# Twenty-one short and fourteen long dummy matmuls in the fill of a fused attention and ReGLU kernel, in place of four and twelve

## Chip, cores, metric

One core of a Trainium2 chip. The metric is the device time of one execution in microseconds (us). The kernel before was run four times: 345.63, 346.99, 349.79 and 351.38 us, median 348.39 us. The profiled execution is the one of 345.63 us.

## What is computed

The reference runs attention on a batch of 8 with 8 heads, 576 positions and 64 features, and feeds the result to a ReGLU feed-forward layer. Attention is the sum of a pooled part (queries, keys and values averaged over groups of 4 positions, full softmax over 144 pooled positions, each result repeated 4 times) and a local part (softmax over the keys less than 4 positions away).

```python
out_up = np.repeat(sm_attn(q_d, k_d, v_d), 4, axis=2)          # q_d, k_d, v_d: means over 4 positions
mask = np.abs(pos[:, None] - pos[None, :]) < 4
out_local = softmax(where(mask, scale * q @ k.T, -1e9)) @ v
x = (out_up + out_local).transpose(0, 2, 1, 3).reshape(4608, 512)
out = (np.maximum(x @ w_gate, 0) * (x @ w_val)) @ w_out        # 512 -> 1536 -> 512
```

## The kernel before

The work is cut into 32 head pairs (two heads of 64 features side by side, 128 rows) for attention and nine chunks of 512 tokens for the feed-forward layer. Each engine runs its instructions strictly in the order in which they are written. That order is not computed at build time: it is a list of words by hand or by a planner, `FRONT` for the fill (the first pairs, until the feed-forward work of chunk 0 can keep TensorE busy), `ORDER` for the repeated middle, `TAIL` for the end. Each word emits one step, and a step's last number is mostly the PSUM bank that it uses (there are eight).

The steps of the fill that matter here, for head pair p:

- `loadq/p`, `loadk/p`, `loadv/p`: the loads, issued by GpSimd (POOL). The first q alone is loaded by SyncE (SP) and cast by ScalarE (ACT).
- `tr/p/i/bank` (L364): TensorE (PE) turns q and k by multiplying with an identity; `ev/p/..A` or `..V` (L378) copies the result out of PSUM on ACT or VectorE (DVE).
- `vd/p/6` (L408): PE pools the values into bank 6, columns 0 to 255; `vc/p/6` (L417): ACT copies them out.
- `s1/p/b` (L427 pooled, L438 local): PE makes the scores in banks b to b+3; `ed/p` (L462) and `ex/p/g` (L448): ACT takes their exponentials; `ma/p/g` (L454): DVE applies the band mask.
- `sd/p/6` (L475): PE makes the pooled attention in bank 6, columns 0 to 259; `rd` (L499) and `td` (L504): DVE divides it into `xo`.
- `su/p/4` (L487): PE makes the local attention in banks 4 and 5; `ru` (L512) and `tu/p/g` (L518): DVE divides it into `xo`.
- `xp/p/g` (L622, L624): PE adds both parts, turned back; `xe` (L634) copies them to `xT`, the input of the feed-forward layer.
- `hg`, `hv` (L639): the first feed-forward matmuls, 128x512 each.
- `warm/n` (L812): n dummy matmuls on zeros. The short ones have 248 columns and write bank 6, columns 264 to 511, which nothing reads. The long ones, emitted once ahead of the list, have 512 columns and write bank 7.

A dummy has no data to wait for, but it does wait for the engines that were still to read its bank: the profile shows the first of the two dummies behind `td/0/6` waiting for that step's DVE instruction, though the columns differ.

Before, there are twelve long dummies at the very beginning, two short ones ahead of `tr/1/0/7` and two short ones ahead of `vd/1/6`.

## Time and profile before

| | |
|---|---|
| median of 4 runs | 348.39 us |
| lowest, highest | 345.63, 351.38 us |
| profiled execution | 345.63 us, of it a span of 343.9 us from the first to the last instruction |
| PE busy | 334.5 us, 3210 matmuls |
| DVE, ACT, POOL busy | 295.9, 218.0, 183.4 us |
| all L812 matmuls | 12 of 512 columns, 4 of 248 |
| PE waits of 0.2 us and more, 0 to 24 us | 4.9 us in eight waits |
| PE waits of 0.2 us and more, 24 to 344 us | 0.9 us in three waits |

A timeline row gives the start, the length from the first start to the last end, engine, source line, operation, tiles, shape, and the number of instructions merged into the row; in brackets stands how long the engine had been idle and what ended that. Matmuls overlap, so the distance between starts, not the length of one, is what a matmul costs in a stream. The PEclk row of the page is the clock that a throttle granted. It stands at 9 in every slice.

### The profile page before, as it was taken

How to read it: one execution, taken by the hardware profiler on the slowest of the kernel's cores; microseconds unless marked ns; L12 is line 12 of the kernel's file. 1: busy time of each engine (PE TensorE's matmuls, PEld its weight loads, DVE VectorE, ACT ScalarE, POOL GpSimd, SP SyncE). 2: the span in 40 equal slices, each digit the busy share in tenths (PEclk: the TensorE clock that was granted, in tenths of full speed). 3: DMA queues.
4: the chain of work that ended last, by engine and by line, in shares of the span. 5: the costliest groups of instructions: out<-in, count | busy, mean ns of one | idle time of the engine just before them, and what ended most of it. 6: DMA issues, size and time to landing. Idle time of an engine off the chain costs nothing.

```text
span 343.9 us, 8224 instructions
## 1 busy us (share of the span) xinstructions
PE 334.5 (97%) x3210; PEld 214.4 (62%) x3210; DVE 295.9 (86%) x546; ACT 218.0 (63%) x423; POOL 183.4 (53%) x232
## 2 busy tenths in 40 slices
PE   7789999999999999999999999999999999999996
PEld 3665556666475756575666556665766557768685
DVE  6695679988999999999999999899999798786892
ACT  4878767767767776677667767776677633334222
POOL 8986547686999695989296877840300000000000
PEclk9999999999999999999999999999999999999999
DMA  9999999999999999999989995992100001001023
GB/s 148 165 171 186 186 192 161 141 172 153 215 147 172 124 170 120 134 158 178 84 105 137 180 128 75 128 170 53 43 20 33 31 2 46 32 31 59 30 66 109
DMA packets 167974, 40.02 MB, mean 116 GB/s; under 512 B 149856, under 2 KB 164864, under 8 KB 167936
## 3 DMA queue, kind: packets, MB, share of 16 engines
q0 software_dynamic: 132160, 22.63, 92.9%
q1 hardware_dynamic: 35632, 16.84, 26.4%
q8 instruction: 25, 0.41, 0.5%
q14 instruction: 13, 0.11, 0.1%
q10 hardware_dynamic: 144, 0.03, 0.1%
HBM read 45.86 MB, written 9.44 MB: 161 GB/s over the span
## 4 chain that ended last, share of the span: by engine, by line
PE 90%; DVE 4%; DMA 2%; ACT 2%; issue 1%; POOL 1%; DVEq 0%; ACTq 0%; POOLq 0%
PE ps L639 48%; PE ps L724 23%; PE ps L905 4%; PE ps L585 4%; PE ps L438 2%; PE ps L427 2%; PE ps L593 2%; PE ps L364 2%; DMA qk<-in_q_dram 2%; PE ps L408 1%; DVE ee L454 1%; DVE gT L651 1%; DVE xn L612 1%; DVE xo L718 0%; DMA out_dram<-y_sb 0%
## 5 line engine op out<-in xcount | busy, mean ns | idle before, releaser
L639 PE MATMUL ps<-xT,wv_sb 128*128 128x512 f16 x432 | 109.1, 379 | 0.0
L639 PE MATMUL ps<-xT,wg_sb 128*128 128x512 f16 x352 | 88.4, 380 | 0.0
L648 ACT ACTIVATE r<-ps 128x512 f16<-128x512 f32 x88 | 52.0, 596 | 31.7 <-PE ps L639 29.2
L651 DVE TENSOR_TENSOR gT<-r,ps 128x512 f16<-128x512 f16 x88 | 59.1, 681 | 7.5 <-PE ps L639 4.7
L639 PEld LDWEIGHTS <-wv_sb 128*128 128x128 f16 x432 | 40.4, 98 | 39.7
L639 PEld LDWEIGHTS <-wg_sb 128*128 128x128 f16 x352 | 32.6, 98 | 32.3 <-issue 0.2
L612 DVE TENSOR_TENSOR xn<-ps,rden 64x720 f16<-64x720 f32 x48 | 43.4, 905 | 5.4 <-ACT rden L608 4.2
L603 ACT ACTIVATE rden<-ps 64x720 f32<-64x720 f32 x48 | 36.7, 764 | 14.4 <-PE ps L593 13.4
L448 ACT ACTIVATE ee<-ps 112x576 f16<-112x576 f32 x64 | 38.7, 647 | 6.0 <-PE ps L438 4.9
L309 POOL DMA_DIRECT2D qk<-in_k_dram x46 | 33.7, 738 | 10.3 <-DMA v<-in_v_dram 3.6
L309 POOL DMA_DIRECT2D qk<-in_q_dram x46 | 33.7, 737 | 8.6 <-DMA v<-in_v_dram 2.1
L724 PEld LDWEIGHTS <-gT 128*128 128x128 f16 x324 | 31.5, 98 | 9.0
L454 DVE TENSOR_TENSOR ee<-ee,cst_sb 112x576 f16<-112x576 f16 x64 | 31.2, 510 | 5.3 <-ACT ee L448 4.8
L724 PEld LDWEIGHTS <-xo 128*128 128x128 f16 x288 | 27.4, 98 | 7.8 <-DVE xo L718 0.3
L334 POOL DMA_DIRECT2D vw<-in_v_dram x30 | 28.6, 953 | 5.6 <-DMA wv_sb<-in_moe_w_val_dram 2.2
L351 DVE TENSOR_REDUCE qkd<-qkT 128x288 f16<-128x1152 f16 x23 | 30.9, 1344 | 0.0
L758 ACT COPY q<-ps 128x256 f32<-128x256 f32 x45 | 16.8, 372 | 21.7 <-PE ps L724 21.4
L386 POOL TENSOR_TENSOR v<-v 72x512 f32<-72x512 f16 x21 | 26.3, 1254 | 4.9 <-DMA v<-in_v_dram 4.3
L724 PE MATMUL ps<-wo_sb,gT 128*128 128x256 f16 x216 | 28.0, 273 | 0.0
L724 PE MATMUL ps<-wt,xo 128*128 128x256 f16 x216 | 27.7, 273 | 0.2 <-DVE xo L718 0.2
L571 DVE TENSOR_TENSOR xT<-xn 128x576 f16<-128x576 f16 x28 | 23.7, 847 | 0.5
L915 ACT COPY vw<-ps 128x256 f32<-128x256 f32 x30 | 10.8, 373 | 20.7 <-PE ps L905 13.8
(108 smaller groups left out, 552.3 us busy)
## 6 DMA issues: line engine op xcount, KB each, us to landing
out_dram<-y_sb SPq DMA_DIRECT2D x24, 256.0 KB, 3.7
vw<-in_v_dram POOLq DMA_DIRECT2D x30, 168.0 KB, 7.2
qk<-in_q_dram POOLq DMA_DIRECT2D x46, 72.0 KB, 6.2
qk<-in_k_dram POOLq DMA_DIRECT2D x46, 72.0 KB, 5.8
v<-in_v_dram POOLq DMA_DIRECT2D x21, 144.0 KB, 7.8
out_dram<-y_sb SPq DMA_DIRECT2D x22, 128.0 KB, 1.7
wg_sb<-in_moe_w_gate_dram POOLq DMA_DIRECT2D x4, 384.0 KB, 9.7
wv_sb<-in_moe_w_val_dram POOLq DMA_DIRECT2D x4, 384.0 KB, 10.8
```

The lines of the kernel that those rows point to most:

```text
L309: nc.gpsimd.dma_start(dst.rearrange("p (j h d) -> p j h d", h=2, d=64)[:, :, hh, :], _dap(src, off + hh * S * D, [[D, 96], [NQ * D, NB], [ ...
L334: nc.gpsimd.dma_start(t, _dap(v, base, [[D, WK], [NQ * D, n], [1, D]]))
L351: nc.vector.tensor_reduce(out=qkd[hp % 2].rearrange("p i t -> p (i t)"), in_=qkT[hp % 4][:, 0 : 2 * S].rearrange("p (t f) -> p t f", f=4), ...
L386: nc.gpsimd.tensor_tensor(out=m, in0=t[:, :, 0:128], in1=t[:, :, 128:256], op=ALU.add)
L448: nc.scalar.activation(out=o, in_=ps[0:WK, p0 + 2 * g : p0 + 2 * g + 2, 0:288], func=AF.Exp, scale=scale)
L454: nc.vector.tensor_tensor(out=o, in0=o, in1=_sap(masks_sb, (0, WK), 288 * g, [[0, 2], [1, 288]]), op=ALU.mult,)
L603: nc.scalar.activation(out=rden[lo : lo + 64], in_=ps[de : de + 64, 4 + 2 * hh : 6 + 2 * hh, 0:360], func=AF.Ln)
L612: nc.vector.tensor_tensor(out=xn[lo : lo + 64], in0=ps[lo : lo + 64, 4 + 2 * hh : 6 + 2 * hh, 0:360], in1=rden[lo : lo + 64], op=ALU.mult,)
L639: nc.tensor.matmul(out=out, lhsT=w[:, kk, bass.ts(jj, 128)], rhs=xT[:, kk, c * TCH : (c + 1) * TCH], start=(kk == 0), stop=(kk == 3),)
L648: nc.scalar.activation(out=r1[j % 3], in_=h1, func=AF.Relu)
L651: nc.vector.tensor_tensor(out=gT[c % 2][:, jj, :], in0=r1[j % 3], in1=h2, op=ALU.mult)
L724: nc.tensor.matmul(out=out, lhsT=left[:, i, :], rhs=right[i], start=(first and i == 0), stop=(i == NK - 1), skip_group_check=True,)
```

## The change

The first call emits fourteen long dummies in place of twelve. In the list, two groups of short dummies grow and six are new; everything else keeps its order, and no instruction of DVE, ACT, POOL or SP is added, removed or moved. Only the words around each group are shown; the rest of the list is only broken into lines at other places.

```diff
-ev/0/00A/2 loadq/3 warm/2 tr/1/0/7
+ev/0/00A/2 loadq/3 warm/5 tr/1/0/7
...
-ev/1/11A/0 loadv/3 sd/0/6
+ev/1/11A/0 loadv/3 warm/1 sd/0/6
...
-td/0/6 wg/0 warm/2 vd/1/6
+td/0/6 wg/0 warm/5 vd/1/6
...
-s1/1/0 wv/0 ma/0/1 ed/1/0 ones/4 su/0/4
+s1/1/0 wv/0 ma/0/1 ed/1/0 ones/4 warm/3 su/0/4
...
-ex/1/0/0 tu/0/0/4 tr/2/1/2
+ex/1/0/0 tu/0/0/4 warm/2 tr/2/1/2
...
-ma/1/0 loadv/4 vc/1/6 s1/2/0
+ma/1/0 loadv/4 vc/1/6 warm/1 s1/2/0
...
-ma/2/1 xe/1/0A/4 s1/3/0
+ma/2/1 xe/1/0A/4 warm/2 s1/3/0
...
-ex/3/0/0 tu/2/1/4 hv/0/0/7
+ex/3/0/0 tu/2/1/4 warm/2 hv/0/0/7
...
-        emit_warm(12, True)
+        emit_warm(14, True)
```

That makes 21 short dummies where there were 4, and 14 long ones where there were 12.

## Prediction

> **What bounds the kernel now.** I read the page first: busy shares, the forty slices, the chain that ended last.

> ```profile
> PE 334.5 (97%) x3210; PEld 214.4 (62%) x3210; DVE 295.9 (86%) x546; ACT 218.0 (63%) x423; POOL 183.4 (53%) x232
> ...
> PE   7789999999999999999999999999999999999996
> ...
> PEclk9999999999999999999999999999999999999999
> ...
> PE 90%; DVE 4%; DMA 2%; ACT 2%; issue 1%; POOL 1%; DVEq 0%; ACTq 0%; POOLq 0%
> ```

> PE ends the kernel; only the first three slices (8.6 us each) have holes. So the fill is worth what it delays the first solid PE work. The list of PE's waits says where the holes are and what happens to a delay later:

> ```profile
> PE ps L812 <- DVE zero_sb L271: 1.3, 1, 1.3
> PE ps L364 <- ACT ee L448: 0.8, 1, 0.8
> PE ps L812 <- DVE xo L504: 0.8, 1, 0.8
> PE ps L364 <- DMA qk<-in_q_dram: 0.6, 1, 0.6
> PE ps L622 <- DVE xo L518: 0.6, 1, 0.6
> PE ps L408 <- DVE xo L504: 0.4, 1, 0.4
> PE ps L585 <- DVE ee L454: 0.4, 1, 0.4
> PE ps L528 <- ACT qkT L378: 0.3, 1, 0.3
> ```

> Longest waits first: no hole is over 1.3 us, and the waits after 24 us add up to 0.9 us. A delay that leaves the fill therefore reaches the end nearly whole.

> Next PE's timeline of the first microseconds, and one row of long matmuls from later.

> ```profile
> 1.26 5.06 PE L812 MATMUL ps<-zero_sb 128*128 128x512 f16 x12 [1.26 <-DVE zero_sb L271]
> 6.54 0.82 PE L364 MATMUL ps<-cst_sb,qk 96*64 96x120 f16 x24 [0.22 <-DMA qk<-in_k_dram]
> 7.40 0.49 PE L408 MATMUL ps<-vw,cst_sb 112*128 112x128 f16 x6
> 7.73 0.38 PE L812 MATMUL ps<-zero_sb 128*128 128x248 f16 x2
> 8.67 0.40 PE L364 MATMUL ps<-cst_sb,qk 96*64 96x120 f16 x8 [0.57 <-DMA qk<-in_q_dram]
> ...
> 11.54 0.37 PE L812 MATMUL ps<-zero_sb 128*128 128x248 f16 x2 [0.80 <-DVE xo L504]
> 11.75 0.50 PE L408 MATMUL ps<-vw,cst_sb 112*128 112x128 f16 x6
> ...
> 30.42 1.89 PE L639 MATMUL ps<-xT,wg_sb 128*128 128x512 f16 x8
> ```

> Twelve long dummies take 5.06 us, 0.42 each. Later the same 512 columns cost (1.89 - 0.39)/7 = 0.21 us (0.39 is one alone). So PE starts at half speed, though the PEclk row shows 9 from the first slice. The 24 tr matmuls take 0.82 us at 6.54, and the same 0.82 at 17.87 and 29.13: from 6.5 us this execution is at full speed and stays there. It is also the fastest of the four runs. The other three, 346.99, 349.79 and 351.38, were not profiled.

> **The change part by part.** A short dummy costs (11.75 - 11.54)/2 = 0.105 us at full speed, 0.21 at half.

> 1. *Two more long ones.* The twelfth began at about 5.93 (6.32, the end, less 0.39) at the new speed, so two more end their turn at 5.93 + 3 x 0.214 = 6.57, 0.03 after tr/0 began. At half speed they would cost 2 x 0.42 = 0.85, and tr/0 would be 0.7 late. What hides that: PE's 0.57 before tr/1 (a DMA's landing), 0.54 of ACT before 9.12, 2.35 of DVE before 10.05. Taken: 0; ends 0 and 0.13 (0.7 less PE's 0.57).
> 2. *Three more ahead of tr/1 (7.73).* Five end at 8.26, the q load lands at 8.6: 0. Without the landing as cover, 0.32.
> 3. *One ahead of sd/0.* It falls into PE's hole between the tr's last start and sd at 10.32, where sd waits for ACT's ed/0; its own wait, for vc/0 on ACT, ended at 8.6. 0; up to 0.1.
> 4. *Three more ahead of vd/1 (11.54).* The group waits for td/0, so it begins where the hole ends; behind it in PE's queue stand vd/1 and s1/1, and ACT stood idle 0.68 us until s1/1 let ed/1 start at 12.79, and then had work without a break to 16.2. 3 x 0.105 = 0.32 on the path; nothing covers it.
> 5. *Three ahead of su/0 and two ahead of tr/2.* su/0 comes 0.32 + 0.32 late, then DVE's ru/0 and tu/0; DVE had waited 0.66 for su/0. tr/2 waits for ACT (14.03, after 0.80 idle), so the two dummies fit into the hole. What is late next: DVE's ev/2 by about 0.15 beyond step 4, into gaps of 0.20 and 0.19. 0; up to 0.3.
> 6. *One ahead of s1/2.* Here a wait is added. These rows are ACT's and PE's timeline:

> ```profile
> 15.19 0.49 ACT L378 CAST qkT<-ps 128x384 f16<-128x384 f32 x1
> ...
> 15.56 0.38 ACT L417 CAST vd<-ps 72x256 f16<-72x256 f32 x1
> 15.73 0.25 PE L427 MATMUL ps<-qkd 64*72 64x144 f16 x2 [0.15 <-ACT qkT L378]
> ...
> 16.33 0.65 ACT L448 ACTIVATE ee<-ps 112x576 f16<-112x576 f32 x1
> ```

> s1/2 starts at 15.73, when ACT's ev/2 (15.19 + 0.49 = 15.68) is done. The dummy writes bank 6, which vc/1 (L417) still reads until 15.94. In the built order the wait on ACT moves from s1/2 to the dummy, and sd/1 loses its own: it is now that of vc/1. So s1/2 starts at 15.94 + 0.05 + 0.105 = 16.10 in place of 15.73, 0.37 late; the turn from one kind of matmul to another costs up to 0.15 more (12.03 to 12.18 between vd/1 and s1/1, where nothing waits). Behind the dummy stand s1/2, sd/1 and su/1; ACT's ex/2 waits for s1/2, DVE's rd/1 for sd/1, and PE's vd/2 for td/1. Taken: 0.43; ends 0.2 and 0.52.
> 7. *Two ahead of s1/3.* 0.21, up to 0.36 with a turn. s1/3 is followed by su/2, whose second pair waits 0.32 for DVE's mask: covered, 0; up to 0.36.
> 8. *Two ahead of hv/0/0.* They wait for td/2 (DVE, 20.54 + 0.42 = 20.96), 0.06 after hv/0 started, then 0.21 more; PE was idle 0.77 before 22.39. 0.

> Other engines' queues issue the same instructions in the same order; POOL's loads of the fill wait for no PE step here.

> Sum for an execution like the profiled one: 0.32 + 0.43 = 0.75 us, so span 343.9 + 0.75 = 344.65 and, with the 1.73 around it, 346.4. That is below the median of before only because the profiled run lies 2.76 below it. Ends: 0 (all in holes) and 0.13 + 0.32 + 0.1 + 0.32 + 0.3 + 0.52 + 0.36 = 2.05 us.

> *The spread.* The edit can lower the median only through executions like 349.79 and 351.38, 4.2 and 5.8 us above the profiled one. If in these PE stays at half speed for longer, the size fits: PE's steps between 6.5 and 24 us take 17.5 - 3.6 = 13.9 us without the waits (4.9 less the first 1.3), and half speed adds at most that, less 3.6 of holes. That is a conclusion from sizes; no row shows such an execution. Two of four were late; with denser PE work I take half as many, one in four (ends: none, two in four). Prompt executions then lie at 346.4 to 347.7 (346.99 + 0.75), and the median, with a quarter late, near the middle: **347.0 us**, 0.4% below 348.39.

> [...] This trace's largest hole after the start is 0.8 us and the clock stays up. [...]

> **The rivals.** A measurement here can tell about 1% from no change, 3.5 us.

> - *A: the spread has another origin* (landing times, the chip) and no execution is at half speed after 8 us. For it: the one trace shows none, and DMA is busy in 9 tenths of the fill. Against: the two groups of two. Each execution then pays 0.75: 348.39 + 0.75 = 349.1.
> - *B, the other side: dummies at half speed.* Where the clock is late anyway, 17 x 0.21 + 0.85 = 4.4 us of dummies run while the slow real work has filled the 3.6 us of holes, so most of it lies on the path in front of the first hv. Late executions go to about 355, and if over half are late the median is 352 or more. It decides at a late share of one half. For it: two of four were late. Against: more PE work should raise the clock earlier.
> - *C: full gain.* The holes take all dummies and no execution is late: 345.6 to 347.0, about 346.0. Faster by over 1% it is only where before's median, taken again, is 349.5 or more. For it: 4.9 us of holes against 1.8 us of dummies. Against: steps 4 and 6.

> **How the numbers follow.** Forecast 0.47 (own range 346.2 to 348.3), A 0.22, B 0.16, C 0.15. The range takes in the forecast, A with the 2.05 us end partly, and C, and leaves out most of B: 345.2 to 350.8. Faster by over 1%: most of C and a fifth of the forecast, where a new median of before is high: 0.22. Slower: B, and a fifth of A: 0.20. The rest, 0.58, within 1%.

> **What would show it.** Step 1: tr/0 near 6.57. Step 4: ed/1 on ACT 0.32 later. Step 6: PE's L812 waiting for ACT's L417, s1/2 about 0.7 later than 15.73. Steps 2, 3, 5, 7, 8: no new wait of ACT or DVE. The first hv about 0.75 later, and the span too. Wrong: a span under 343.9, a delay over 2.05 us with the clock up at 6.6, or a spread of the after runs as wide as before's.

## The result, and the profile after

The kernel after takes 346.83 us (median of 35 runs, 345.71 to 349.14), the kernel before 348.23 us (56 runs, 345.02 to 356.22). The ratio of the two is 0.9989 (95% interval 0.9973 to 1.0006). It is formed without the executions that lie over 1.5% above their kernel's fastest; before has such executions, after has none, which is why the medians differ by more than the ratio. So for the executions that go well no change is shown, and the ones that go badly are gone from after's. The prediction was 347.0, within 1%.

The first lines are from the page of the kernel after (span 344.6 us, device time 346.32 us).

```profile
PE 336.9 (98%) x3229; PEld 215.8 (63%) x3229; DVE 296.0 (86%) x546; ACT 218.1 (63%) x423; POOL 182.5 (53%) x232
...
PE   8899999999999999999999999999999999999996
...
PEclk9999999999999999999999999999999999999999
...
PE 88%; DVE 4%; ACT 3%; DMA 2%; issue 1%; POOL 1%; DVEq 0%; ACTq 0%; POOLq 0%
```

PE's first three slices are fuller by a tenth each, and PE is busy 2.4 us longer; the rest is as before. PE's list of waits:

```profile
PE ps L812 <- DVE xo L504: 0.8, 1, 0.8
PE ps L408 <- DVE xo L504: 0.4, 1, 0.4
PE ps L812 <- ACT vd L417: 0.4, 1, 0.4
PE ps L585 <- DVE ee L454: 0.3, 1, 0.3
PE ps L364 <- ACT ee L448: 0.3, 1, 0.3
PE ps L528 <- ACT qkT L378: 0.3, 1, 0.3
```

The wait for ACT ahead of tr/2 fell from 0.8 to 0.3, because dummies stand in it. The wait of a dummy (L812) for ACT's L417 is new: it is the one foreseen ahead of s1/2. After 24 us PE waits 0.6 us (the L585 and L528 rows) in place of 0.9. PE's timeline shows where each group stands:

```profile
1.26 5.75 PE L812 MATMUL ps<-zero_sb 128*128 128x512 f16 x14 [1.26 <-DVE zero_sb L271]
6.94 0.82 PE L364 MATMUL ps<-cst_sb,qk 96*64 96x120 f16 x24
...
8.11 0.69 PE L812 MATMUL ps<-zero_sb 128*128 128x248 f16 x5
8.92 0.40 PE L364 MATMUL ps<-cst_sb,qk 96*64 96x120 f16 x8
...
11.79 0.69 PE L812 MATMUL ps<-zero_sb 128*128 128x248 f16 x5 [0.80 <-DVE xo L504]
12.31 0.50 PE L408 MATMUL ps<-vw,cst_sb 112*128 112x128 f16 x6
...
16.55 0.27 PE L812 MATMUL ps<-zero_sb 128*128 128x248 f16 x1 [0.40 <-ACT vd L417]
16.75 0.25 PE L427 MATMUL ps<-qkd 64*72 64x144 f16 x2
...
31.45 1.89 PE L639 MATMUL ps<-xT,wg_sb 128*128 128x512 f16 x8
```

The last row stood at 30.42 before: the fill is 1.03 us longer. Of that, 0.25 is the load of q: tr/1 starts at 8.92 in place of 8.67 because the load, issued at 3.25 in place of 3.27, landed at 8.88 in place of 8.63. That start lies anywhere between 8.06 and 9.56 in the profiles of the experiments below, and in a second profile of after's kernel at 8.86, so I take the 0.25 as chance. The other 0.78 is the change. The span grew by 0.7: PE's waits after 24 us give back 0.3.

### The profile page after: what moved, and what is told of

It reads as the page before. It is cut to its first block, busy times and chain, and to the rows that moved or that the text cites. A ratio compares the mean times of both kernels' runs of the same rounds, so it can differ in the third digit from the quotient of the medians.

```text
span 344.6 us, 8261 instructions
## 1 busy us (share of the span) xinstructions
PE 336.9 (98%) x3229; PEld 215.8 (63%) x3229; DVE 296.0 (86%) x546; ACT 218.1 (63%) x423; POOL 182.5 (53%) x232
## 4 chain that ended last, share of the span: by engine, by line
PE 88%; DVE 4%; ACT 3%; DMA 2%; issue 1%; POOL 1%; DVEq 0%; ACTq 0%; POOLq 0%
PE ps L639 46%; PE ps L724 22%; PE ps L905 4%; PE ps L585 3%; PE ps L438 2%; PE ps L427 2%; PE ps L593 2%; DMA qk<-in_q_dram 2%; PE ps L364 2%; DVE xn L612 1%; PE ps L408 1%; ACT rden L603 1%; DVE ee L454 1%; DVE gT L651 1%; DVE xo L718 1%
## 5 line engine op out<-in xcount | busy, mean ns | idle before, releaser
L639 PE MATMUL ps<-xT,wv_sb 128*128 128x512 f16 x432 | 109.0, 379 | 0.0
L639 PE MATMUL ps<-xT,wg_sb 128*128 128x512 f16 x352 | 88.4, 380 | 0.0
L639 PEld LDWEIGHTS <-wv_sb 128*128 128x128 f16 x432 | 40.5, 98 | 39.7
L639 PEld LDWEIGHTS <-wg_sb 128*128 128x128 f16 x352 | 32.6, 98 | 32.3 <-issue 0.2
L448 ACT ACTIVATE ee<-ps 112x576 f16<-112x576 f32 x64 | 38.7, 647 | 6.4 <-PE ps L438 5.4
L454 DVE TENSOR_TENSOR ee<-ee,cst_sb 112x576 f16<-112x576 f16 x64 | 33.2, 539 | 5.4 <-ACT ee L448 4.8
L386 POOL TENSOR_TENSOR v<-v 72x512 f32<-72x512 f16 x21 | 25.2, 1202 | 2.3 <-DMA v<-in_v_dram 1.7
L608 ACT ACTIVATE rden<-rden 128x720 f32<-128x720 f32 x28 | 22.5, 803 | 0.7
```

What stands on the lines that cost most here:

```text
L386: nc.gpsimd.tensor_tensor(out=m, in0=t[:, :, 0:128], in1=t[:, :, 128:256], op=ALU.add)
L448: nc.scalar.activation(out=o, in_=ps[0:WK, p0 + 2 * g : p0 + 2 * g + 2, 0:288], func=AF.Exp, scale=scale)
L454: nc.vector.tensor_tensor(out=o, in0=o, in1=_sap(masks_sb, (0, WK), 288 * g, [[0, 2], [1, 288]]), op=ALU.mult,)
L639: nc.tensor.matmul(out=out, lhsT=w[:, kk, bass.ts(jj, 128)], rhs=xT[:, kk, c * TCH : (c + 1) * TCH], start=(kk == 0), stop=(kk == 3),)
```

## The experiments

Every execution has its span and its mean granted clock on record. Both are in the tables, since the question is whether the long times come from the clock. I count 0.998 to 1.000 as full speed throughout (the profiled executions of before and after read 1.000). The record of a profiled execution gives the moments of change as well: before rose at 5.94 us and stayed up to 343.86, that is 337.92 us or 99 times 3.413; after rose at 6.47 and stayed up to 344.39, again 337.92 us. The record begins with this first rise: before's mean reads 1.000, and its PEclk row 9, although its dummies ran at half speed until 5.94 (0.42 us each, against 0.21 for 512 columns later). So a mean well below 1 tells of time at half speed after a first rise, not of a late rise. In the fallen executions that were profiled the rises and falls lie on such a grid of 3.41 us too (first kernel: 5.14, 11.97 and 35.86, two and seven times 3.41 apart), and the first rise, which places the grid, came at 4.81 us in the eighth kernel and at 6.50 in the third. As an estimate, one such stretch at half speed makes 3.41/2/345 = 0.005 in the mean clock: 0.995 is one stretch, 0.985 three, 0.976 five, 0.966 seven. The profiled ones show five stretches at 0.976 (third kernel) and seven at 0.966 (first).

The theory: the upper half of before's times comes from the clock, and dummies hold it. The rival: landing times of DMAs.

**Only the start**, the first kernel:

```diff
-        emit_warm(12, True)
+        emit_warm(14, True)
```

> Fourteen long dummies, the four short ones of before. Theory (the upper tail of before comes from TensorE's clock coming late or dropping again in the fill, and dense dummy work prevents it): if the start decides, prompt executions as before (about 345.6 to 347), few or none over 350, and the mean granted clock is below 1 only in the late ones. If the short dummies decide, the tail stays (a quarter and more over 350). Rival (the tail has another origin, landing times of DMAs): the tail stays and the granted clock is 1.000 in the late executions too.

**Only the short ones**, the second: after's list with `emit_warm(12, True)`.

> Twelve long dummies, the twenty-one short ones of after. Theory, if the short dummies hold the clock: no execution over 350, median near after's 346.8. If the start decides: a tail as before's, the median near 348. Rival (DMA landings): a tail as before's, with the granted clock at 1.000.

**No short ones**, the third:

```diff
-ev/0/00A/2 loadq/3 warm/2
+ev/0/00A/2 loadq/3
...
-td/0/6 wg/0 warm/2 vd/1/6
+td/0/6 wg/0 vd/1/6
```

> Twelve long dummies and no short one. Theory: the holes of the fill are empty, the clock drops more often, so the late executions become the common ones: median 350 or more, with a mean granted clock below 1.000 that goes with the time. Rival (short dummies only cost time, the tail has another origin): the median is up to 0.4 below before's, and the spread is before's.

**After's without the two groups that were priced**, the fourth:

```diff
-td/0/6 wg/0 warm/5 vd/1/6
+td/0/6 wg/0 warm/2 vd/1/6
...
-loadv/4 vc/1/6 warm/1 s1/2/0
+loadv/4 vc/1/6 s1/2/0
```

> After's kernel without the two groups that I priced: three of the five dummies ahead of vd/1 and the one ahead of s1/2 are taken out. If 0.32 and 0.43 are what they cost, the first hv of a prompt execution starts 0.75 earlier than after's at an equal landing of q, the span is 0.3 to 0.75 shorter than after's, and the median about 346.1 to 346.5, with no tail if the other dummies suffice to hold the clock. Rival (the two groups are what holds the clock): some executions at 350 and more come back.

Measured; before's executions come from the three chips on which the experiments ran. In the last column are the executions at full clock alone.

| kernel | median us | executions | clock under 0.99 | clock 0.994 or 0.995 | median at full clock |
|---|---|---|---|---|---|
| before | 348.52 | 82 | 42 | 1 | 346.38 |
| after | 346.80 | 36 | 0 | 1 | 346.77 |
| fourteen long only | 350.65 | 12 | 7 | 1 | 347.0 |
| short ones only | 346.75 | 12 | 0 | 0 | 346.75 |
| no short ones | 351.27 | 6 | 6 | 0 | none |
| without the two groups | 346.77 | 12 | 1 | 1 | 346.49 |

The rival falls. Of before's 82 executions the 39 at full clock lie between 344.81 and 348.05 us, the 42 under 0.99 between 347.55 and 388.67, and with the mean clock the time goes: 347.55 to 350.13 at 0.985, 350.86 to 352.83 at 0.974 to 0.976, 353.77 to 357.16 at 0.966. The extreme is one execution of the first kernel at 0.653 and 494.45 us. The clock is not all of the spread: 350.05 us in the first kernel and 349.89 in the sixth come at 0.999, and nothing here shows what made them long. The two long dummies by themselves do not stop the falls (7 of 12); the short ones alone do all that the change does (0 of 12).

The page of the first kernel (span 355.0 us), as profiled, shows such an execution; the PEclk row now has a dent:

```profile
PE   7799999998999999999999999999999999999996
...
PEclk9655999999999999999999999999999999999999
```

PE's row gives no hint: its slices 2 to 4 are 7, 9, 9 where before's are 7, 8, 9, since at half speed the same work reads as busier (eight L364 matmuls of that execution: 0.40 us at 9.20, 0.61 at 28.46). The same execution, by three of its 3.41 us stretches; after the bounds come PE, PEld, DVE, ACT and POOL busy, the granted clock, DMA share and GB/s:

```profile
5.14:8.55 3.41, 2.36 (x36) 1.45 (x35) 1.35 (x7) 0.63 (x4) 3.41 (x4) 1.00 2.40 154
8.55:11.97 3.42, 2.25 (x54) 1.57 (x51) 1.06 (x5) 2.89 (x9) 3.42 (x6) 1.00 2.46 155
11.97:15.38 3.41, 2.85 (x36) 2.35 (x36) 1.35 (x5) 2.03 (x5) 3.41 (x6) 0.50 2.52 157
```

The clock was up at 5.14, stayed up through two stretches, and was halved at 11.97, after a stretch in which PE was busy for 2.25 of 3.42 us; no wait in it or reaching out of it was longer than 0.8 us. It came back at 35.86, seven stretches later, when the long feed-forward matmuls were under way. So nothing was late about the rise; the clock fell again. No fallen execution of before itself was profiled; that its low means are falls after a first rise follows from what the mean counts.

The fourth kernel answers the question of the prices. These rows are the first xp/2 in before, in after and in this kernel:

```profile
22.39 0.28 PE L622 MATMUL ps<-cst_sb,xo 72*128 72x288 f16 x1 [0.55 <-DVE xo L518]
...
23.42 0.28 PE L622 MATMUL ps<-cst_sb,xo 72*128 72x288 f16 x1 [0.24 <-DVE xo L518]
...
21.89 0.28 PE L622 MATMUL ps<-cst_sb,xo 72*128 72x288 f16 x1 [0.22 <-DVE xo L518]
```

From tr/1 to the first xp/2, which takes the landing of q out, it takes 21.89 - 8.13 = 13.76 us, before 22.39 - 8.67 = 13.72, after 23.42 - 8.92 = 14.50. The two groups cost 0.74 us of the fill, 0.75 was predicted. The whole time shows less of it: the profiled span is 0.5 shorter than after's, as expected, but the median of 346.77 misses the expected 346.1 to 346.5 and equals after's; at full clock it is 346.49. One of its twelve executions fell to 0.949 (354.6 us), which after's own kernel did in none of 48; that the dummies taken out also protect is possible, but one execution does not show it, and it was not profiled.

**Early groups alone, later groups alone**, the fifth and sixth:

```diff
 # early: fourteen long, and of after's short groups only
+loadq/3 warm/5   warm/1 sd/0/6   wg/0 warm/5 vd/1/6
 # late: fourteen long, before's two groups (2 and 2), and
+warm/3 su/0/4   warm/2 tr/2/1/2   warm/1 s1/2/0   warm/2 s1/3/0   warm/2 hv/0/0/7
```

> Fourteen long dummies and the three early groups of after (five ahead of tr/1, one ahead of sd/0, five ahead of vd/1); the five groups from su/0 on are left out. Theory: the clock falls at the end of a 3.41 us window in which TensorE is busy too little (2.25 us and 2.11 us in the windows that fell, 2.36 us and more in those that did not), and the windows with the least work lie between 6.5 and 13 us. Then the early groups alone hold it: no execution over 350, mean clock 0.995 and more, and, without the 0.43 us of the wait ahead of s1/2, a median of about 346.4. Rival (the later groups are needed): a tail as before's, a quarter and more over 350 with a clock of 0.985 and less.

> Fourteen long dummies, the two early groups as before (two and two), and the five later groups of after. Theory: the thin windows before 13 us stay thin, the clock falls as often as before: a third or more of the executions over 349.5 with a clock of 0.985 and less; those that stay up pay 0.43. Rival (the later groups hold the clock): no tail, median 346.5 to 347.

| kernel | median us | executions | clock under 0.99 | clock 0.995 | median at full clock |
|---|---|---|---|---|---|
| early groups | 346.55 | 12 | 0 | 0 | 346.55 |
| late groups | 347.1 | 12 | 0 | 3 | 346.84 |

The early groups hold the clock, as expected, but the reason given there, too little busy time, does not hold: the profiled execution stayed up after a stretch with 2.07 us busy, less than the 2.25 and 2.11 that fell, and through a wait of 1.34 us. The expectation of the late ones was wrong: no execution is under 0.99. Three are at 0.995 (346.94, 347.97 and 348.22 us), which is one stretch at half speed where before's fallen executions mostly spend three to seven. The likely reading is that the clock still falls now and then, since the groups between 7 and 12 us are before's own, and that dummies between 12 and 22 us bring it back in the next stretch; none of those three was profiled, so this is argued and not shown.

**Thin dummies**, the eighth: as many, as long and at the same places as after's, on 32 rows and 32 columns of weights in place of 128 and 128.

```diff
-                out=ps[:, 7, :] if wide else ps[:, 6, 264:512],
-                lhsT=zero_sb[:, 0:128],
-                rhs=zero_sb[:, 128 : 640 if wide else 376],
+                out=ps[:, 7, :] if wide else ps[0:32, 6, 264:512],
+                lhsT=zero_sb[:, 0:128] if wide else zero_sb[0:32, 0:32],
+                rhs=zero_sb[:, 128:640] if wide else zero_sb[0:32, 128:376],
```

> After's kernel with short dummies on 32 rows and 32 columns of the array in place of 128 and 128: as many, as long (248 columns each), at the same places. If the gate counts the time in which TensorE has work, they hold the clock as after's do: no execution under 0.99, median 346.8. If it counts how much of the array works, they do nothing: a third or more of the executions under 0.99 and over 349.5, as in before.

Median 356.74 us (355.66 to 358.88), all six executions with a fallen clock; ratio to before 1.0305 (1.0263 to 1.0346). They take the time of dummies and did not hold the clock in any of the six. The stretches of its profiled execution, in the columns of the last such view:

```profile
8.22:11.64 3.42, 3.11 (x60) 2.24 (x60) 0.85 (x3) 2.69 (x8) 3.42 (x5) 1.00 2.43 155
11.64:15.05 3.41, 2.83 (x44) 1.94 (x44) 1.59 (x6) 2.28 (x6) 3.41 (x5) 1.00 2.41 157
15.05:18.46 3.41, 3.35 (x47) 2.67 (x49) 2.85 (x7) 2.34 (x8) 3.41 (x6) 0.50 1.55 194
```

PE was busy 2.83 us in the stretch after which the clock fell. Two stretches with less and no fall, before's least busy one and one of the early groups' kernel:

```profile
12.76:16.18 3.42, 2.47 (x60) 2.17 (x60) 2.69 (x8) 3.38 (x9) 3.42 (x6) 1.00 2.27 165
...
4.54:7.95 3.41, 2.07 (x29) 1.04 (x28) 1.34 (x16) 0.61 (x1) 3.41 (x5) 1.00 2.31 152
```

Busy time therefore does not part the two: the clock fell after 2.83 us and stayed after 2.47 and 2.07. Another measure, an estimate worked out from the trace's matmuls, is the array share: each one's columns times 0.214/512 us, after the (1.89 - 0.39)/7 = 0.214 us that 512 columns cost in before's row of L639 (twice that at half clock, after the dummies' 0.42), times its rows and columns of weights as shares of a full dummy's 128 and 128, summed over a stretch and divided by 3.41. A matmul that reaches over the end of a stretch is divided between the two. The stretches at full clock up to 24 us in twelve profiled executions:

| outcome | array share |
|---|---|
| clock fell at the end | 0.28 (thin), 0.32 (fourteen long only), 0.35 (no short ones) |
| clock stayed | 0.34 (thin, 8.22 to 11.64), all others 0.38 and more |
| before, the three thinnest | 0.45, 0.39, 0.38, stayed |
| after, the three thinnest | 0.47, 0.48, 0.50, stayed |

But for one stretch at 0.34, a bound near 0.36 parts these stretches. The rest of the twelve traces agrees: at the very end, where the last work runs out, the clock fell after stretches with 0.345 (short ones only), 0.24 and less, and it stayed through one with 0.39 (late groups, from 340.7 us) and one with 0.40 (bank 1, the seventh kernel below, from 89.0 us).

Before's profiled execution sat just above the bound; a grid with another phase sits below. How often, its own trace tells, if all phases are equally likely: 40% of them give before's execution a stretch under 0.35, and 58% one under 0.36; 42 of 82 fell. For after's none does; for the early groups 1 and 9%, and 0 of 12 fell; for the late ones 14 and 17%, and 3 of 12 lost one stretch. This is an estimate from one trace of each kernel. The one fall of the fourth kernel stays unexplained: no phase puts its trace under 0.39.

For the rise the same measure parts the stretches of these executions as well. In the twelve profiled ones, the stretches ahead of the first rise counted as at half clock, it stayed at half after every stretch with a share of 0.71 and less, and rose after every one with 0.80 and more; in between, one with 0.735 was followed by a rise and one with 0.744 (first kernel, 29.03 to 32.44) was not.

**A version for the holes**, the seventh: twelve long; five ahead of tr/1, one ahead of sd/0; six that write bank 1, free by then, and so run while PE waits for td/0; none ahead of vd/1 and s1/2; five ahead of tr/2, behind su/0.

```diff
-ev/0/00A/2 loadq/3 warm/2
+ev/0/00A/2 loadq/3 warm/5
...
-sd/0/6 ev/1/21V/1
+warm/1 sd/0/6 ev/1/21V/1 warmb/6
...
-td/0/6 wg/0 warm/2 vd/1/6
+td/0/6 wg/0 vd/1/6
...
-tu/0/0/4 tr/2/1/2
+tu/0/0/4 warm/5 tr/2/1/2
...
+    def emit_warm_b(n):
...
+                out=ps[:, 1, 0:248],
```

> A version that fills the holes without standing in the way: twelve long, five ahead of tr/1, one ahead of sd/0, six behind sd/0 that write bank 1 (free since DVE's ev/1), so that they run while TensorE waits for td/0, none ahead of vd/1, five ahead of tr/2 behind su/0, none later. If 0.32 and 0.43 are prices of place and the clock needs only busy windows: no execution over 350, the thinnest window about 2.9 us busy, the fill as short as before's or 0.2 shorter, the median 345.6 to 346.3, below after's 346.83. Rival (the dummies cost wherever they stand, or bank 1 brings a new wait): 346.8 and more.

It was run once more, with after beside it on the same chip.

> After's kernel once more, on the chip of the next two, so that they can be compared: median 346.8, no execution with a mean clock under 0.99, where before's has them in about half.

> The kernel with six dummies in bank 1 and none ahead of vd/1 and s1/2, once more beside after's: if it saves the 0.74 us that after's two groups cost in the fill, its median is 0.4 to 0.9 below after's on the same chip (345.8 to 346.3); rival: the later stages take it back, and both are equal within 0.2.

| kernel | median us | executions | clock under 0.99 | clock 0.994 or 0.995 | median at full clock | ratio to before |
|---|---|---|---|---|---|---|
| bank 1, first | 345.82 | 12 | 0 | 1 | 345.76 | 0.9974 (0.9940 to 1.0007) |
| bank 1, again | 345.70 | 12 | 0 | 1 | 345.57 | 0.9986 (0.9954 to 1.0018) |
| after, again | 347.22 | 12 | 0 | 1 | 347.2 | 1.0001 (0.9966 to 1.0036) |

PE's timeline of the second run:

```profile
10.22 0.80 PE L822 MATMUL ps<-zero_sb 128*128 128x248 f16 x6
10.93 0.50 PE L408 MATMUL ps<-vw,cst_sb 112*128 112x128 f16 x6
...
12.37 0.69 PE L812 MATMUL ps<-zero_sb 128*128 128x248 f16 x5
```

The 0.80 us hole ahead of vd/1 is gone: the six dummies (L822) fill it and vd/1 follows at once. From tr/1 to the first xp/2 it takes 13.51 us (13.50 in the first run), 0.2 less than before, as expected. Its median is 1.5 us under after's on the same chip, where 0.4 to 0.9 was expected, and 1.9 us under before's there (347.58, 24 runs). The fill explains 14.50 - 13.51 = 0.99 of the 1.5; after's 347.22 in that run, above the expected 346.8, is part of the rest. It has the lowest median here; that its executions at full clock beat before's is likely, but both intervals reach 1.

## Why the prediction was right, point by point

- *Steps 1 to 3, no cost.* Right. The clock rose at 6.47 in place of 5.94, so tr/0 began at 6.94 and not at 6.57; the load of q covered it. From tr/1 to sd/0 it is 1.65 us in both kernels.
- *Step 4, 0.32.* From tr/1 to vd/1: 3.08 before, 3.39 after, 0.31.
- *Step 5, covered.* From tr/1 to tr/2 0.31 more, nothing beyond step 4.
- *Step 6, 0.43 by a new wait.* From tr/1 to s1/2: 7.06 before, 7.83 after; less 0.31, 0.46. The wait for L417 is in the list.
- *Steps 7 and 8, covered.* The first xp/2 is 0.78 late, 0.01 more than steps 4 and 6 together. The first hv itself is later than the 0.75 given as a sign: from tr/1 to it 12.23 before (20.90 - 8.67) and 13.32 after (22.24 - 8.92), 1.09 more. PE's wait ahead of xp/2, which was 0.55 by its row and not 0.77, shrank to 0.24 and took up the difference.
- *"A delay that leaves the fill therefore reaches the end nearly whole."* Over-sized. Of 1.03 us 0.7 reached the end of the profiled one, whose later waits shrank by 0.3, and executions at full clock are 346.77 - 346.38 = 0.39 us apart (95% interval about 0 to 0.95, by resampling).
- *The spread.* "Two of four were late" was a fair sample: 42 of 82. "I take half as many, one in four" was too many: none of 48 executions of after is under 0.99, two are at 0.995. This is the mis-sized term. It came with a wrong picture, a clock that comes late: in the three fallen executions that were profiled it comes in time, at 4.81 to 6.50 us, and falls again.
- *The rivals.* A falls with the clock column, B too (no late execution is left; its "more PE work should raise the clock earlier" is not shown: the first rise was at 6.47 us in after's profiled execution, at 5.94 in before's), and of C only the half holds that no execution is late; the dummies of steps 4 and 6 do cost.

The prediction says of before's trace that its largest hole after the start is 0.8 us and the clock stays up. Holes of that size do not tell which way it goes: in the first kernel's profiled execution the clock fell with PE busy for 2.25 of 3.42 us and no wait over 0.8. Nor did the two long dummies hold it by themselves (7 of 12 fell with before's four short ones).

The two errors, more late executions than there are and a higher price, point the same way: both made the forecast too slow. That 347.0 still lies within 0.2 of the measured 346.83 is because a median hardly feels how many executions are late as long as they are fewer than half, and because the price is small. That half of the four runs were late, as half of all are, was luck.

## What to carry to other kernels

Look at the spread of the times and at each execution's mean clock before reading one profile: the profiled execution may be one that does not have the problem. In this fill, where TensorE's work is thin for some microseconds, dummies on 128 by 128 kept its clock up (with after's groups 0 of 48 executions are under 0.99, with before's 42 of 82), those on 32 by 32 did not (6 of 6 fell). They belong where nothing waits behind them: in a bank whose readers are done, not behind a wait that the next real step needs (13.51 us from tr/1 to the first xp/2 against after's 14.50). Count in array share per 3.41 us, not in busy time: here the clock fell after 2.83 us busy at a share of 0.28, and stayed after 2.07 us busy at one of 0.38 or more.
